# A 12-tile mLSTM attention woven into a mixture of experts: the opening's order on GpSimd and VectorE is changed, and tiles 4 to 11 get two more units between their steps

## The chip, the cores and the metric
The kernel runs on one core of a Trainium2 chip. The metric is the device time of one execution in microseconds (us), as the median of several runs. TensorE (PE) does matmuls and transposes, ScalarE (ACT) activations and copies, VectorE (DVE) elementwise work, GpSimd (POOL) masks and clears, SyncE (SP) starts the DMAs.

## The reference
Three layers follow one another over 1536 tokens (2 batches of 768) with 320 features:

```python
# 1. mLSTM attention, 8 heads of 40, for every step t
m_new = np.maximum(f_gate[:, :, t] + m, i_gate[:, :, t])
f_stab = np.exp(f_gate[:, :, t] + m - m_new)
i_stab = np.exp(i_gate[:, :, t] - m_new)
C = f_stab[:, :, None, None] * C + i_stab[:, :, None, None] * np.einsum('bhd,bhe->bhde', vt, kt)
n = f_stab[:, :, None] * n + i_stab[:, :, None] * kt
y[:, :, t] = o * (C @ q) / np.maximum(np.abs(n . q), 1.0)      # o = sigmoid(o_gate)
# 2. MoE 1: Sinkhorn-normalised gates P (8 rounds), dense over 8 experts
h = np.maximum(x @ w1[e], 0.0);  out += P[:, e:e + 1] * (h @ w2[e])
# 3. MoE 2: the same sizes, top-1 expert of each token by softmax
```

## The kernel before
**Attention in 12 tiles.** Attention is done in its chunked form, in tiles of 128 tokens that alternate between the two batches. `attn(i)` is a Python generator; each `yield` ends one step of a tile. In order, a tile's steps are: `pw`, two matmuls that spread the gates (L239, from a gate tile `gl_` and a tile `R` that VectorE makes in `make_R`, L211), whose result ScalarE turns into the decay weights `W` (relu L244, exp L245) and GpSimd masks (L246); the transposes of q and of k (`turn`, L225, copied out by ScalarE at L229); the scores `sc` (L262); the product of scores and `W` on VectorE (L268); `pn`, weights times v (L274, two steps of four heads each); `pi`, query times state (L291), with the chain `num` on VectorE that divides and gates (L292 to L302); `pc`, the state's increment (L308); the transposes of the tile's result x (L336, L337), copied as a high part `xh` by ScalarE (L341, L345), with the low part `xl` by VectorE (L346, L347); the update of the state `cbd` (L324, L325).

**MoE 1 in items.** The two layers of an expert are split into a high and a low part of each operand, so a product takes three matmuls. An item is one expert on two or four tiles: eight `s1_unit`s (eight matmuls each, L477 to L485, ScalarE's relu `hh` L486, VectorE's `hl` L487) and then `s2_mm` (L492 to L494). Expert weights come in by DMA as `raw` chunks; `split_chunk` makes a high part `w1h` or `w2h` on ScalarE (L461) and a low part `w1l` or `w2l` on VectorE or GpSimd (L465).

**What sets the order.** The program is emitted under a manual schedule: the order of the Python calls is the order on each engine, and an engine takes its instructions in that order. Tiles 0 and 1 (`f0`, `f1`, with `lead=True`) run in the opening by explicit `steps(...)` calls. Tiles 2 to 11 run inside items 0 to 4, which have 144 units; a unit is half an `s1_unit` or six `s2_mm` matmuls. After each unit `bg_early(u)` takes one step of each running generator. A hand-written table gives the unit at which a tile's `pw` is emitted, and `make_R` for it is emitted two units earlier, after the steps of that unit:

```python
AT = {5: 2, 9: 3, 20: 4, 30: 5, 40: 6, 50: 7, 58: 8, 66: 9, 74: 10, 82: 11}
if u + 2 in AT:
    make_R(AT[u + 2])
if u in AT:
    g = attn(AT[u]); next(g); active.append(g)
```

`GT` starts the gate scans of later chunks (`gates(c)`, L146 to L170 on VectorE), `DT` the decays (L180, L187, L188), `OT` the sigmoids of o (`sigmoid_o`: it loads the sigmoid table at L98, does two tiles at L101, and loads the exp table again at L104). `keep_warm(n, cols)` emits n matmuls on zeros that nothing reads. `emit_const` and `emit_const1` clear and mask constants on GpSimd.

Of the kernel before, what the change touches and what calls it, by code (L numbers as in the profile page):

```python
# [18 lines left out]
def mlstm_moe_moe_kernel(ctx, tc, q, k, v, i_gate, f_gate, o_gate, wg1, w1a, w2a, wg2, w1b, w2b, out):  # L19
    nc = tc.nc  # L20
    pe, act, dve, pool, sp = nc.tensor, nc.scalar, nc.vector, nc.gpsimd, nc.sync
# [13 lines left out]
    def f32(ap):  # L35
        return ap.bitcast(F32)
# [46 lines left out]
    gl_ = atp.tile([128, S], F32R, name="gl_")  # L83
# [21 lines left out]
        yield  # L105

    def emit_const():
        pool.memset(mask, 0.0)
        for t in range(4):
            pool.affine_select(out=mask, in_=mask, pattern=[[-1, 2 * H]], compare_op=ALU.not_equal, fill=1.0, base=-32 * t, channel_multiplier=1)  # L110
        pool.memset(ident, 0.0)
        pool.affine_select(out=ident, in_=ident, pattern=[[-1, 128]], compare_op=ALU.not_equal, fill=1.0, base=0, channel_multiplier=1)
        for t in range(2):
            for w in (qs, ks):
                pool.memset(w[t][:, :, D:64], 0.0)
        pool.memset(f32(gl_), 1.0)
        for t in ku:
            pool.memset(t[:, :, D:64], 0.0)
        dve.memset(gx, 1.0)
        dve.memset(wgr2[0:64, 2], 0.0)  # L120
        dve.memset(msk, 1.0)
        dve.memset(msk[:, 0:1], 0.0)
        for t in vs:
            dve.memset(t[:, :, D:D + 1], 1.0)

    def emit_const1():
        for w in (qs, ks):
            pool.memset(w[2][:, :, D:64], 0.0)
        for t in cbd:
            pool.memset(t, 0.0)  # L130
        pool.memset(one, 1.0)
        pool.memset(fold, 0.0)
        for t in range(2):
            pool.affine_select(out=fold, in_=fold, pattern=[[-1, E]], compare_op=ALU.not_equal, fill=1.0, base=-E * t, channel_multiplier=1)
# [41 lines left out]
    def decays(c0, c1):  # L176

        Gv = G.rearrange("p (c t) -> p c t", t=L)
        n = c1 - c0
        dve.tensor_tensor(out=gend[:, c0:c1], in0=Gv[:, c0:c1, L - 1:L].to_broadcast([R16, n, 2 * H]),  # L180
                          in1=mask[0:R16].unsqueeze(1).to_broadcast([R16, n, 2 * H]), op=ALU.mult)
        yield
        yield
        yield
        p = pst()
        for c in range(c0, c1):
            pe.transpose(p[:, (c - c0) * R16:(c - c0 + 1) * R16], G[:, c * L:(c + 1) * L], ident[0:R16, 0:R16])  # L187
        pe.matmul(p[:, 256:256 + n * R16], one, gend[:, c0:c1].rearrange("p c h -> p (c h)"), start=True, stop=True)  # L188
        act.activation(out=dq[:, c0:c1].rearrange("p c h -> p (c h)"), in_=p[:, 0:n * R16], func=AF.Exp)
        act.activation(out=dec[:, c0:c1].rearrange("p c h -> p (c h)"), in_=p[:, 256:256 + n * R16], func=AF.Exp)  # L190
# [4 lines left out]
    def keep_warm(n, cols=512):  # L195

        for _ in range(n):
            pe.matmul(warm_p[:, 0:cols], warm[:, 0:128], warm[:, 0:cols], start=True, stop=True)
# [16 lines left out]
    def attn(i, ps=pst, lead=False):  # L215
# [6 lines left out]
        def turn(src, dst):  # L222
            pq = ps()
            for p in range(4):
                pe.transpose(pq[:, p * L:(p + 1) * L], src[:, 2 * p:2 * p + 2, :].rearrange("s a d -> s (a d)"), ident)  # L225
            if i == 1 and dst is kT:
                dve.tensor_copy(dst.rearrange("p a t -> p (a t)"), pq)
            else:
                act.copy(out=dst.rearrange("p a t -> p (a t)"), in_=pq)  # L229
# [18 lines left out]
        if c < NCH - 1:  # L248
            u = ku[i % 2]
# [4 lines left out]
        if not lead:  # L254
            turn(qs[j], qT)
            yield
            turn(ks[j], kT)
            yield
        sc = [ps(), ps()]
        for p in range(4):  # L260
            for a in range(2):
# [6 lines left out]
            dve.tensor_tensor(out=Wv, in0=sc[a].rearrange("s (p t) -> s p t", t=L), in1=Wv, op=ALU.mult)  # L268
        yield
        yield  # L270
        pn = ps()
        for a in range(2):
            for h in range(a, H, 2):
                pe.matmul(pn[:, h * V:(h + 1) * V], W[:, h, :], vs[j][:, h, :], start=True, stop=True)  # L274
                if lead:
                    keep_warm(1, 256)
            yield
        num = atp2.tile([128, H, V], F32, tag="num", name="num")
        nf = num.rearrange("t h d -> t (h d)")
# [79 lines left out]
    def load_rows(dst, src):  # L359

        sp.dma_start(out=dst[:, 0:2], in_=src[0:256, :].rearrange("(a p) f -> p a f", p=128))
        sp.dma_start(out=dst[0:64, 2], in_=src[256:320, :])
        sp.dma_start(out=dst[64:128, 2], in_=src[256:320, :])
# [4 lines left out]
    def split_wg():  # L368
        act.copy(out=wgs[:, :, 0:E], in_=wgr)
        dve.tensor_tensor(out=wgs[:, :, E:2 * E], in0=wgr, in1=f32(wgs[:, :, 0:E]), op=ALU.subtract)  # L370
# [58 lines left out]
    def load_chunk():  # L429
        n = nload[0]  # L430
        if n >= len(chunks):
            return
        e, w, t = chunks[n]
        r = raw.tile([128, FF], F32, tag="raw", name="raw")
        if w == "w1" and t < 2:
            sp.dma_start(out=r, in_=w1a[e, t * 128:(t + 1) * 128, :])
        elif w == "w1":
            sp.dma_start(out=r[0:64], in_=w1a[e, 256:320, :])
            sp.dma_start(out=r[64:128], in_=w1a[e, 256:320, :])
        else:  # L440
            k0, k1 = 3 * t, min(3 * t + 3, NF)
            sp.dma_start(out=r[:, 0:(k1 - k0) * DM].rearrange("p (k d) -> p k d", d=DM),
                         in_=w2a[e, k0 * 128:k1 * 128, :].rearrange("(k p) d -> p k d", p=128))
        raws[n] = r
        nload[0] += 1

    def split_chunk(eng=None, wait=False):

        n = nsplit[0]
        if n >= len(chunks):  # L450
            return
        e, w, t = chunks[n]
        if eng is None:
            eng = dve if e < 3 else pool
        r = raws.pop(n)
        if w == "w1":
            rv, h, l = r, w1h[:, t, :], w1l[:, t, :]
        else:
            k0, k1 = 3 * t, min(3 * t + 3, NF)
            rv, h, l = r[:, 0:(k1 - k0) * DM].rearrange("p (k d) -> p k d", d=DM), w2h[:, k0:k1, :], w2l[:, k0:k1, :]  # L460
        act.copy(out=h, in_=rv)  # L461
        nsplit[0] += 1

        def low():
            eng.tensor_tensor(out=l, in0=rv, in1=f32(h), op=ALU.subtract)  # L465
            load_chunk()
        if wait:
            return low
        low()
# [519 lines left out]
    with tc.manual_schedule():  # L989
# [15 lines left out]
        load_chunk()  # L1005
        drain(gates(0))
        g1 = gates(1)
        emit_const1()
        alt = [0]

        def psx():
            alt[0] += 1
            return ps1() if alt[0] % 2 else ps2()
        f0, f1 = attn(0, pst, True), attn(1, psx, True)
        make_R(0)
        make_R(1)

        def steps(*fs):
            for f in fs:
                next(f)  # L1020
        steps(f0, f0, f1, f0, f1)
        steps(f0, g1, g1)
        steps(f1)
        steps(f0, f0)
        steps(f1, f1)
        steps(g1, g1)
        low = split_chunk(wait=True)
        for t in range(2):
            act.activation(out=so[t], in_=so[t], func=AF.Sigmoid)
# [1 line left out]
        keep_warm(3)  # L1031
        steps(f0, f0, f0)
        steps(f1)
        low()
        steps(f0)
        keep_warm(2)
        steps(f1, f1, f1)
        steps(f0)
        steps(f1)
        low = split_chunk(wait=True)  # L1040
        steps(f0)
        steps(f1)
        steps(f1)
        low()
        split_chunk()
        keep_warm(2)
        load_tile(3, "o")
        active = [g1, g1]
# [8 lines left out]
        def bg_early(u):  # L1057
            for g in list(active):
                if next(g, "end") == "end":
                    active.remove(g)  # L1060
            if u % 2 == 1 and slow:
                if next(slow[0], "end") == "end":
                    slow.pop(0)
            if u in GT:
                active.append(gates(GT[u]))
            if u in DT:
                active.append(decays(DT[u], DT[u] + 1))
            if u == 8:
                load_rows(wgr, wg1)
                sp.dma_start(out=wgr2[:, 0:2], in_=wg2[0:256, :].rearrange("(a p) f -> p a f", p=128))  # L1070
                sp.dma_start(out=wgr2[64:128, 2], in_=wg2[256:320, :])
            if u == 20:
                split_wg()
            if u in OT:
                active.append(sigmoid_o(OT[u]))
            if u == 3:
                active.extend((f0, f1))
# [3 lines that stand above are left out]
                g = attn(AT[u])  # L1081
                next(g)
                active.append(g)
            for blk, at_ in ((0, 24), (1, 66), (2, 97)):
                if u == at_:
                    active.append(logits(wgs, blk))
            if u == 100:
                slow.append(sinkhorn())

        units = [0]  # L1090
# [100 lines left out]
```

## Time and profile before
| what | value |
|---|---|
| median of 3 runs | 1002.5 us (1001.16 to 1004.19) |
| the profiled execution's own time | 1005.57 us |
| its span in the trace | 1003.9 us |
| TensorE busy | 970.8 us (97%) |
| VectorE busy | 483.0 us (48%) |
| ScalarE busy | 358.0 us (36%) |
| GpSimd busy | 202.7 us (20%) |
| mean granted TensorE clock | 0.985 of full speed |

The busy times are those of the traced span. The granted clock is a share of 2.4 GHz; 0.50 is 1.2 GHz. A row of the timeline has the start, the duration, engine, line, operation, output and input tiles with their shape, and in brackets how long the engine stood idle ahead of it and what released it.

### The profile page before, as it was taken

What the parts mean: (1) busy time and instruction counts of PE and PEld (TensorE: products, weight loads), DVE (VectorE), ACT (ScalarE), POOL (GpSimd) and SP (SyncE); (2) the same over time, 40 slices, a digit from 0 to 9 for tenths busy, and PEclk for the clock granted to TensorE, in tenths of its full rate; (3) what the DMA queues carried; (4) which work ended last, traced back from release to release, by engine and by line L of the source; (5) the groups of instructions that cost most, each with busy time, mean ns of one, the idle gap of its engine ahead of it and who ended that gap; (6) DMA issues with size and microseconds to landing.
All of it is one profiled execution on the core that took longest, in us unless ns stands there. A gap on an engine that the chain in (4) does not pass through costs nothing. (4 is left out here: it accounts for less than half of the span.)

```text
span 1003.9 us, 14450 instructions
## 1 busy us (share of the span) xinstructions
PE 970.8 (97%) x5633; PEld 856.5 (85%) x5633; DVE 483.0 (48%) x1089; ACT 358.0 (36%) x585; POOL 202.7 (20%) x206
## 2 busy tenths in 40 slices
PE   7898999999999999999999999999999998899997
PEld 5888788888999888899998888999888986788885
DVE  8655865565523422222222222222225468687773
ACT  5644565222312232113113211311332134567772
POOL 3212121001000022004002200500221112365552
PEclk9798999999999999999999999999999999899999
DMA  9722621200321405002101200210100034788772
GB/s 196 162 49 37 158 59 50 65 19 1 95 105 55 146 24 182 36 1 61 55 1 35 82 1 1 76 41 1 34 1 27 20 94 133 225 233 245 238 231 76
DMA packets 91366, 84.11 MB, mean 84 GB/s; under 512 B 54237, under 2 KB 81887, under 8 KB 91296
## 3 DMA queue, kind: packets, MB, share of 16 engines
q1 hardware_dynamic: 89088, 76.42, 27.3%
q0 software_dynamic: 2208, 6.75, 1.9%
q8 instruction: 45, 0.74, 0.3%
q14 instruction: 25, 0.20, 0.1%
HBM read 79.21 MB, written 4.76 MB: 84 GB/s over the span
## 5 line engine op out<-in xcount | busy, mean ns | idle before, releaser
L486 ACT ACTIVATE hh<-s 128x512 fp32r<-128x512 f32 (+1 forms) x200 | 116.1, 580 | 446.8 <-PE s L485 446.7
L492 PE MATMUL s<-w2h,hh 128*128 128x320 f32 x832 | 262.7, 316 | 0.0
L493 PE MATMUL s<-w2l,hh 128*128 128x320 f32 x832 | 258.0, 310 | 0.0
L494 PE MATMUL s<-w2h,hl 128*128 128x320 f32 x832 | 258.0, 310 | 0.0
L487 DVE SCALAR_TENSOR_TENSOR hl<-s,hh 128x512 fp32r<-128x512 f32 (+1 forms) x200 | 133.8, 669 | 217.1 <-ACT hh L486 216.7
L492 PEld LDWEIGHTS s<-w2h,hh 128*128 128x128 f32 x832 | 157.2, 189 | 2.0
L493 PEld LDWEIGHTS s<-w2l,hh 128*128 128x128 f32 x832 | 157.2, 189 | 1.5 <-DVE w2l L840 0.2
L494 PEld LDWEIGHTS s<-w2h,hl 128*128 128x128 f32 x832 | 157.0, 189 | 0.0
L534 DVE SCALAR_TENSOR_TENSOR acc<-s,probs,acc 128x320 f32<-128x320 f32 x76 | 41.8, 551 | 188.7 <-PE s L494 188.7
L465 POOL TENSOR_TENSOR w1l<-raw,w1h 128x1024 fp32r<-128x1024 f32 x15 | 35.8, 2418 | 390.3 <-ACT w1h L461 390.3
L477 PE MATMUL s<-xh,w1h 128*128 128x512 f32 (+1 forms) x200 | 79.9, 400 | 0.4 <-DVE es L666 0.4
L482 PE MATMUL s<-xl,w1h 128*128 128x512 f32 (+1 forms) x200 | 79.8, 399 | 0.0
L483 PE MATMUL s<-xh,w1l 128*128 128x512 f32 (+1 forms) x200 | 77.9, 390 | 0.8 <-DVE w1l L465 0.8
L485 PE MATMUL s<-xh,w1l 128*128 128x512 f32 (+1 forms) x200 | 78.1, 390 | 0.6 <-DVE w1l L465 0.6
L478 PE MATMUL s<-xl,w1h 128*128 128x512 f32 (+1 forms) x200 | 77.9, 389 | 0.2 <-DVE xl L346 0.2
L480 PE MATMUL s<-xh,w1h 128*128 128x512 f32 (+1 forms) x200 | 77.7, 388 | 0.0
L484 PE MATMUL s<-xh,w1h 128*128 128x512 f32 (+1 forms) x200 | 77.5, 387 | 0.0
L479 PE MATMUL s<-xh,w1l 128*128 128x512 f32 (+1 forms) x200 | 77.5, 387 | 0.0
L485 PEld LDWEIGHTS s<-xh,w1l 128*128 128x128 f32 x200 | 38.2, 191 | 9.4 <-DVE w1l L465 0.8
L477 PEld LDWEIGHTS s<-xh,w1h 128*128 128x128 f32 x200 | 38.2, 191 | 9.0 <-DVE es L666 0.8
L483 PEld LDWEIGHTS s<-xh,w1l 128*128 128x128 f32 x200 | 38.1, 190 | 8.9 <-DVE w1l L465 1.0
L480 PEld LDWEIGHTS s<-xh,w1h 128*128 128x128 f32 x200 | 38.1, 191 | 8.5
(303 smaller groups left out, 1428.8 us busy)
## 6 DMA issues: line engine op xcount, KB each, us to landing
raw<-in_moe_w_dram SPq DMA_DIRECT2D x44, 320.0 KB, 3.3
raw<-in_moe_w_dram SPq DMA_DIRECT2D x54, 256.0 KB, 4.2
w2raw<-in_moe_w_dram SPq DMA_DIRECT2D x17, 640.0 KB, 5.4
raw<-in_moe_w_dram SPq DMA_DIRECT2D x20, 512.0 KB, 3.6
raw<-in_moe_w_dram SPq DMA_DIRECT2D x20, 480.0 KB, 3.8
wr<-in_moe_w_dram SPq DMA_DIRECT2D x8, 1024.0 KB, 8.3
q<-in_q_dram SPq DMA_DIRECT2D x12, 160.0 KB, 3.8
k<-in_k_dram SPq DMA_DIRECT2D x12, 160.0 KB, 3.9
```

Source lines behind the costliest of these rows:

```text
L477: pe.matmul(p, w1h[:, 0, fs], xh_[:, 0, cols], start=True, stop=False)
L478: pe.matmul(p, w1h[:, 0, fs], xl_[:, 0, cols], start=False, stop=False)
L479: pe.matmul(p, w1l[:, 0, fs], xh_[:, 0, cols], start=False, stop=False)
L480: pe.matmul(p, w1h[:, 1, fs], xh_[:, 1, cols], start=False, stop=False)
L482: pe.matmul(p, w1h[:, 1, fs], xl_[:, 1, cols], start=False, stop=False)
L483: pe.matmul(p, w1l[:, 1, fs], xh_[:, 1, cols], start=False, stop=False)
L485: pe.matmul(p, w1l[:, 2, fs], xh_[:, 2, cols], start=False, stop=True)
L486: act.activation(out=hh[:, ft, 0:n], in_=p, func=AF.Relu)
L487: dve.scalar_tensor_tensor(out=hl[:, ft, 0:n], in0=p, scalar=0.0, in1=f32(hh[:, ft, 0:n]), op0=ALU.max, op1=ALU.subtract)
L492: pe.matmul(p[:, 0:DM], hh[:, ft, ts], w2h[:, ft, :], start=(first and ft == 0), stop=False)
L493: pe.matmul(p[:, 0:DM], hh[:, ft, ts], w2l[:, ft, :], start=False, stop=False)
L494: pe.matmul(p[:, 0:DM], hl[:, ft, ts], w2h[:, ft, :], start=False, stop=(ft == NF - 1))
```

## The change
`gl_` is cleared first on GpSimd instead of after the pads; `emit_const1` (clears of tile 2's pads, of the states, and a small mask) moves behind the weight masks of tiles 0 and 1; the gate steps of chunk 1 that stood between the two tiles' products, and the low parts of the first weight chunks, take other places in the opening; the matmuls on zeros inside the two lead tiles' `pn` are left out. Tiles 4 to 11 get one more empty step ahead of `sc` and one more ahead of `pn`, so all their later steps come one and then two units later. The logits and the Sinkhorn rounds start two units later.

```diff
     def emit_const():
+        pool.memset(f32(gl_), 1.0)
         pool.memset(mask, 0.0)
...
-        pool.memset(f32(gl_), 1.0)
...
             turn(ks[j], kT)
             yield
+            if i > 3:
+                yield
         sc = [ps(), ps()]
...
         yield
         yield
+        if i > 3:
+            yield
         pn = ps()
         for a in range(2):
             for h in range(a, H, 2):
                 pe.matmul(pn[:, h * V:(h + 1) * V], W[:, h, :], vs[j][:, h, :], start=True, stop=True)
-                if lead:
-                    keep_warm(1, 256)
...
         g1 = gates(1)
-        emit_const1()
...
         steps(f1)
+        emit_const1()
         steps(f0, f0)
         steps(f1, f1)
-        steps(g1, g1)
         low = split_chunk(wait=True)
...
         steps(f1)
+        steps(f0)
         low()
-        steps(f0)
         keep_warm(2)
         steps(f1, f1, f1)
         steps(f0)
         steps(f1)
+        split_chunk()
+        steps(f0)
         low = split_chunk(wait=True)
-        steps(f0)
         steps(f1)
         steps(f1)
         low()
-        split_chunk()
...
-            for blk, at_ in ((0, 24), (1, 66), (2, 97)):
+            for blk, at_ in ((0, 24), (1, 68), (2, 99)):
...
-            if u == 100:
+            if u == 102:
                 slow.append(sinkhorn())
```

The line numbers in the rows of the changed order below are one to two higher than in the kernel before (L270 is the product of L268, L278 the `pn` of L274, L338 the transposes of L336, L348 the low part of L346, L467 that of L465, L494 to L496 the matmuls of L492 to L494).

VectorE in the opening, from the products of tiles 0 and 1 to the third low part, before:

```order
L268 TENSOR_TENSOR W<-a,W 128x4x128 x2
L156 TENSOR_TENSOR acc<-acc 16x128
L158 SCALAR_TENSOR_TENSOR acc<-acc 16x128
L268 TENSOR_TENSOR W<-s_309,W 128x4x128
L268 TENSOR_TENSOR W<-s_310,W 128x4x128
L465 TENSOR_TENSOR w1l<-raw,w1h 128x1024
L286 COPY num<-a 128x8
```

And with the change:

```order
L270 TENSOR_TENSOR W<-a,W 128x4x128 x2
L270 TENSOR_TENSOR W<-s_309,W 128x4x128
L270 TENSOR_TENSOR W<-s_310,W 128x4x128
L288 COPY num<-a 128x8
L289 TENSOR_TENSOR num<-a,o_102 128x8x40
L297 SCALAR_TENSOR_TENSOR den<-num 128x8
L298 TENSOR_SCALAR den<-den 128x8
L299 RECIPROCAL den<-den 128x8
L301 TENSOR_TENSOR x<-num,den 128x320
L467 TENSOR_TENSOR w1l<-raw,w1h 128x1024
```

The two gate steps (L156, L158) have gone from between the products, and the first low part stands behind tile 0's chain instead of ahead of it. The second low part, which stood behind both tiles' `xl`, now stands ahead of them, and the third alone behind them.

TensorE around tile 9's `pw` (unit 66, the L239 row), before; the L336 and L337 rows are the transposes of tile 7's x, the L274 rows tile 8's `pn`:

```order
L336 MATMUL a<-ident,x 128x128 x2
...
L274 MATMUL a<-v_101,W 128x41 x4
L492 MATMUL s_1507<-w2h,hh 128x320
L493 MATMUL s_1507<-w2l,hh 128x320
L494 MATMUL s_1507<-w2h,hl 128x320
L492 MATMUL s_1507<-w2h,hh 128x320
L493 MATMUL s_1507<-w2l,hh 128x320
L494 MATMUL s_1507<-w2h,hl 128x320
L274 MATMUL a<-v_101,W 128x41 x4
L239 MATMUL a<-R,gl__110 128x512 x2
```

And with the change, at the same unit; the L338 row is the first of the transposes of tile 7's x:

```order
L338 MATMUL a<-ident,x 128x128 x2
L339 MATMUL a<-ident,x 64x128
L494 MATMUL s_1476<-w2h,hh 128x320
...
L494 MATMUL s_1476<-w2h,hh 128x320
L495 MATMUL s_1476<-w2l,hh 128x320
L496 MATMUL s_1476<-w2h,hl 128x320
L239 MATMUL a<-R,gl__110 128x512 x2
L494 MATMUL s_1476<-w2h,hh 128x320
L495 MATMUL s_1476<-w2l,hh 128x320
L496 MATMUL s_1476<-w2h,hl 128x320
```

Tile 8's `pn` has gone behind tile 9's `pw`, and the transposes of tile 7's x, which stood four units ahead of that `pw`, stand two units ahead of it: twelve matmuls of MoE 1 are all that is left between them.

VectorE over the same units, before, from tile 7's low part to the R of tile 9:

```order
L346 TENSOR_TENSOR xl_69<-a,xh_66 128x2x128
L347 TENSOR_TENSOR xh_66<-a,xh_66 64x128
L156 TENSOR_TENSOR acc<-acc 16x128
L487 SCALAR_TENSOR_TENSOR hl<-s_1474,hh 128x512
L325 TENSOR_TENSOR cbd_107<-cbd_107,a 40x4x41 x2
L268 TENSOR_TENSOR W<-a,W 128x4x128 x2
L158 SCALAR_TENSOR_TENSOR acc<-acc 16x128
L160 CAST gx<-acc 16x128
L211 TENSOR_TENSOR R<-gx,mask 128x1024
```

And with the change:

```order
L348 TENSOR_TENSOR xl_69<-a,xh_66 128x2x128
L349 TENSOR_TENSOR xh_66<-a,xh_66 64x128
L270 TENSOR_TENSOR W<-a,W 128x4x128 x2
L160 CAST gx<-acc 16x128
L211 TENSOR_TENSOR R<-gx,mask 128x1024
```

Tile 7's low part, tile 8's product and tile 9's R now stand in one unit (64), one right behind the other.

## Rows read from the trace of the kernel before
**Rows 1.** The page: busy time of the engines, share of the span, instructions.
```profile
PE 970.8 (97%) x5633; PEld 856.5 (85%) x5633; DVE 483.0 (48%) x1089; ACT 358.0 (36%) x585; POOL 202.7 (20%) x206
```
**Rows 2.** Waits of TensorE, 76 to 190 us: total, times, longest.
```profile
PE a L274 <- issue: 2.0, 3, 1.1
PE a L274 <- DVE W L268: 2.0, 3, 1.1
PE a L239 <- ACT W L244: 1.5, 2, 0.7
PE a L262 <- ACT kT L229: 1.2, 2, 0.8
```
**Rows 3.** Timeline of VectorE in the opening.
```profile
4.86 0.92 DVE L160 CAST gx<-acc 16x128 fp32r<-16x128 f32 x1
...
13.50 0.52 DVE L156 TENSOR_TENSOR acc<-acc 16x128 f32<-16x128 f32 x1
14.05 0.41 DVE L158 TENSOR_TENSOR_SCAN acc<-acc 16x128 f32<-16x128 f32 x1
...
22.67 2.36 DVE L465 TENSOR_TENSOR w1l<-raw,w1h 128x1024 fp32r<-128x1024 f32 x2
24.95 0.21 DVE L160 CAST gx<-acc 16x128 fp32r<-16x128 f32 x1
...
28.16 1.22 DVE L211 TENSOR_TENSOR R<-gx,mask 128x1024 fp32r<-128x1024 f32 x1
```
**Rows 4.** Timeline of GpSimd: the clears of the states in `emit_const1`.
```profile
5.02 0.69 POOL L130 MEMSET cbd<- 128x328 f32 x2
```
**Rows 5.** Timeline of TensorE in the opening.
```profile
25.08 0.58 PE L485 MATMUL s<-xh,w1l 128*128 128x256 f32 x1 [0.62 <-DVE w1l L465]
...
29.43 0.72 PE L239 MATMUL a<-R,gl__110 128*128 128x512 f32 x2 [0.63 <-DVE R L211]
```
**Rows 6.** Windows: us, busy of PE, PEld, DVE, ACT, POOL; granted clock; DMA.
```profile
15.00:25.00 10.00, 8.36 (x74) 7.08 (x72) 8.46 (x22) 5.43 (x10) 0.00 (x0) 1.00 1.07 199
25.00:28.20 3.20, 3.12 (x14) 3.12 (x15) 2.13 (x10) 0.77 (x2) 0.00 (x0) 0.50 1.14 266
35.40:42.00 6.60, 6.45 (x27) 5.59 (x27) 4.53 (x10) 5.21 (x11) 2.60 (x5) 0.50 0.39 90
86.30:93.10 6.80, 6.80 (x32) 6.69 (x31) 3.60 (x9) 0.38 (x1) 0.00 (x0) 0.50 0.00 0
```
**Rows 7.** Timeline of TensorE, tiles 9 to 11.
```profile
137.67 1.06 PE L274 MATMUL a<-v,W 128*128 128x41 f32 x8 [1.12 <-DVE W L268]
...
165.33 0.38 PE L336 MATMUL a<-ident,x 128*128 128x128 f32 x2
...
165.81 0.30 PE L493 MATMUL s<-w2l,hh 128*128 128x320 f32 x1
...
166.38 0.31 PE L494 MATMUL s<-w2h,hl 128*128 128x320 f32 x1
...
171.47 0.71 PE L239 MATMUL a<-R,gl__110 128*128 128x512 f32 x2
```
**Rows 8.** Timeline of VectorE: tile 9's low part to tile 11's R.
```profile
166.41 0.43 DVE L346 TENSOR_TENSOR xl<-a,xh 128x256 fp32r<-128x256 f32 x1 [3.48 <-ACT xh L345]
...
167.15 0.66 DVE L325 TENSOR_TENSOR cbd<-cbd,a 40x164 f32<-40x164 f32 x2
167.82 1.29 DVE L268 TENSOR_TENSOR W<-a,W 128x512 f32<-128x512 f32 x2
169.03 1.22 DVE L211 TENSOR_TENSOR R<-gx,mask 128x1024 fp32r<-128x1024 f32 x1
```
**Rows 9.** Timeline of ScalarE: weights of tile 5, load of the exp table.
```profile
76.03 0.60 ACT L244 ACTIVATE W<-a 128x512 f32<-128x512 f32 x1 [2.17 <-PE a L239]
...
77.85 0.63 ACT L245 ACTIVATE W<-W 128x512 f32<-128x512 f32 x1
...
167.54 1.28 ACT L104 ACT_TABLE_LOAD   x1
```

## The prediction
> **What bounds the kernel now.** The page comes first: TensorE is busy 97% of the span, VectorE 48%, ScalarE 36%, GpSimd 20% [rows 1]. So time is lost or won where TensorE idles or runs at half its clock. Its waits come next. From 76 us to 190 us, the stretch of tiles 5 to 11, four kinds of wait make 6.7 us: `pn` with no releaser shown (2.0), `pn` for the product of scores and weights (2.0), the scores for the copy of kT (1.2) and `pw` for the relu of the `pw` ahead of it (1.5) [rows 2]. In the opening it waits for VectorE's third `w1l` (0.62) and for tile 2's R (0.63) [rows 5]. The windows show what those waits do to the clock: 25.0 to 28.2 us, 35.4 to 42.0 us and 86.3 to 93.1 us run at 0.50, that is at 1.2 GHz [rows 6], so up to 1.6, 3.3 and 3.4 us are lost there (half of each stretch, since the same matmuls take half as long at 2.4 GHz).
>
> All of the change lies in the first 190 us. What is gained or lost there moves the end by as much, since MoE 1 runs on TensorE from there on.
>
> **The opening.** Four edits act on VectorE, which is the engine that TensorE waits for here.
> (1) The cast L160 of chunk 0 takes 0.92 us at 4.86 while GpSimd clears the states at 5.02 (0.69 us), and 0.21 us at 24.95 with nothing on GpSimd [rows 3, 4]. With `emit_const1` moved away, the gate chain, R and `pw` start earlier by some 0.5 us (the cast's 0.71, of which about 0.2 lay under the scan ahead of it in the pipeline; estimate).
> (2) L156 and L158 (0.52 and 0.41) leave the place between the products [rows 3]. They come back behind the third `w1l`, ahead of tile 2's R. Tile 1's product then waits for GpSimd's mask instead, so I take 0.7 at that point, not 0.93.
> (3) The pair of low parts (2.36 for two, so 1.18 each [rows 3]) no longer stands whole behind tile 1's `xl`. The second fits in while VectorE waits for x of tile 1; this brings the third forward by 1.18.
> (4) On the other side tile 0's chain now waits for the sigmoids, which ScalarE still makes at the same place, and tile 1's copy `xh` waits behind one more `w1h` cast.
> Followed row by row with the durations of before, the third `w1l` ends at 23.4 us instead of 25.03, and R of tile 2 at about 28.4 instead of 29.38 (28.16 + 1.22 [rows 3]), because the two gate steps now lie ahead of it. So the sum for the opening is -1.0 us. Its bounds: -2 if the chain moves by all of (1) and (3), and +0.5 from contention, as the moved clears would now run beside tile 0's product and chain, whose cost is bounded below by nothing and above by the 0.71 of edit (1).
>
> Leaving out sixteen matmuls on zeros costs TensorE nothing in itself; they stand where it would wait for VectorE anyway, which is busy 8.46 of 10 us there [rows 6]. But they are activity. In 15 to 25 us TensorE was busy 8.36 of 10 us at clock 1.00 and the clock fell to 0.50 only at 25.0 [rows 6]. The Trainium skill ("TensorE: Matmul & The Clock Gate", Part 1) says that the throttled clock is the default and activity releases it, which speaks against leaving them out. No row of before shows the opening without them. If the clock falls some microseconds sooner, the x transposes and the first matmuls of item 0 run at half clock: about +1.5 us by the 1.6 of the stretch that is there now. I put nothing into the sum and +1.5 into the range.
>
> Of the moved clears the skill has another rule ("SBUF — State Buffer", SBUF: two separate sides): VectorE with two inputs in SBUF is blocked only by a GpSimd operation that reads SBUF. By it the clears, which only write, would cost the chain's two-input steps nothing, and the opening would be -1.0 either way; that L160, a one-input cast, was slowed by clears [rows 3, 4] agrees with its other half.
>
> **The extra steps of tiles 4 to 11.** What they remove: the waits of `pn` and of the scores, 2.0 + 2.0 + 1.2 = 5.2 us of the 6.7 [rows 2], since the copies and the product get one more unit, about 0.9 us (six matmuls at 0.14, from 165.81 to 166.38 for four [rows 7]).
>
> What they add follows from the offsets. A tile's product comes at AT+6 instead of AT+5, its x transposes at AT+14 instead of AT+12. AT itself is not moved, and R for tile i+1 is still made two units ahead of its `pw`.
> - **Tiles 9 to 11.** AT is spaced by 8 there. So x of tile i-1 (AT+14 of that tile), the product of tile i (AT+6) and R of tile i+1 (AT-2) all fall into one unit, in this order on VectorE. `pw` of tile i+1 is two units later. The chain has been traced: x transposes of tile 9 start at 165.33 [rows 7], then `xh`, `xl` at 166.41, the state's 0.66, the product, and R ends at 170.25 (169.03 + 1.22) [rows 8]; without the state's addition, which moves behind, 4.92 - 0.66 = 4.26 us. In before TensorE had four units and two halves of `pn` to do meanwhile, and arrived at `pw` at 171.47 [rows 7]. Now it has the transposes (0.35) and twelve matmuls (12 x 0.143 = 1.72, or eight of `s1`, about 1.87), 2.1 us. It then waits 4.26 - 2.1 = 2.1 us. For tile 10 the decays' matmuls lie between (about 0.4): 1.7. For tiles 9 and 11 the exp table's load (1.28, just behind the second sigmoid [rows 9]) now stands on ScalarE directly ahead of `xh`, and holds it by 0.7 to 1.1: 3.2 and 2.8. Together 7.7 us. In exchange `pn`'s waits there go (1.12 at 137.67 [rows 7], and three more of 0.2 to 0.6, 2.2 in all).
> - **Tiles 4 to 6.** Spacing is 10. The chain `num` of tile i now comes one unit after `pw` of tile i+1 (AT+11), where ScalarE has four activations of `W` to do, 76.03 to 78.48 [rows 9], and MoE 1's `hh` stands behind them, `hl` behind that, `num` behind `hl`. So the x transposes, which had no wait before, wait: 1.0 to 1.3 us each by hand, 3.6 for three.
> - **Tile 8** comes at a spacing of 8 behind 7, and its `pw` meets the same chain in part: 1.4. Some waits stay (0.9 of tile 5's `pn`, 0.3 around tile 6, 0.4 at a k turn): 1.6.
> Sum of the waits after: 7.7 + 3.6 + 1.4 + 1.6 = 14.3, against 6.7. Waits in a row are not fully additive, since TensorE's standing still lets ScalarE and VectorE catch up; I take 2 off: +5.5. Bounds: +3 (each of the R waits 1.5 smaller, as with a shorter hold by the table) and +8.
>
> The logits and Sinkhorn rounds move by two units and still end ahead of unit 143; SyncE's loads move by one or two units with what precedes them. Nothing waits for either, so I cost them at nothing; without that slack each unit would be some 0.9 us.
>
> **Sum.** -1.0 + 5.5 = +4.5 us. The profiled execution took 1005.57 us, 3.1 above the median, so by it 1010.1; against the median of 1002.5, on which I forecast, 1007.0.
>
> **Rivals.**
> - **The waits just go** (faster). If the R chain is ready in time (in before, `pw` of tile 11 came 1.2 us after its R, 171.47 [rows 7] against 170.25), the change gives -5.2, the clock stays up in 86 to 93 us (-3.4) and the opening gives -1.0: 1002.5 - 9.6 = 993. With half of it, 998. Against it stands the arithmetic of two units. The point from which it decides is whether twelve matmuls can last longer than the chain of 4.26.
> - **Offsets cancel** (no change). The x waits are half as long and the table load does not hold `xh`: the waits after are 8 to 9 us, the opening takes 1 off: 1002 to 1004.
> - **The clock falls too** (slower still). The waits of about 3 us are followed by falls to 0.50, as the shorter ones of before seem to be, each stretch costing 1.6 to 3.4 [rows 6]. Against it: TensorE has more than 10 us of work between two such waits. With one or two more: 1009 to 1014.
> - **Only the opening counts** (the extra steps trade like for like, but the clock falls sooner without the zeros): 1002.5 + 1.5 - 1.0 = 1003.
>
> **How the numbers follow.** About 0.3%, 3 us, is what a measurement of this kernel can tell from no change: below 999.5 is faster, above 1005.5 slower. The new waits as forecast hold 0.45, with their own range of 1003 to 1010; the clock falling too 0.10; cancelling 0.17 and the opening alone 0.08; the waits just going, whole or in half, 0.20. Slower takes the third case and three quarters or more of the forecast, 0.50 in sum; no change the rest of it and the two middling ones, 0.30; faster 0.20. The range reaches from half of the first rival, 997, to the upper end of the third, 1013.
>
> **What would show it.** Right: `pw` (L239) waiting for R in three or four places with some 2 to 3 us each near 134 to 165 us; x transposes waiting for x of tiles 4 to 6; no wait of `pn` for the product in tiles 9 to 11; the last L485 of the first `s1_unit` near 23.5 us instead of 25.08, L160 in 0.2 us. Wrong: R ready ahead of `pw` in tiles 9 to 11, or a clock of 1.00 all through 80 to 100 us.

## The result and the profile after

The changed kernel takes 1015.61 us (median of 4, 1011.32 to 1016.14) against 1001.99 us before (4 runs): a ratio of 1.0123, interval 1.0091 to 1.0156. Measured once more among the experiments, it took 1010.75 us against 1002.02 us, ratio 1.0077 (1.0046 to 1.0107). It is slower, as was forecast, by 13.6 and 8.7 us between the medians (about 12 and 8 us by the ratios) where 4.5 were forecast. The first median lies above the stated range (997 to 1013), the second in it. Every difference in this document is below 2% of the time; a gain or a loss is called one only where its interval leaves out 1.

The profiled execution, of 1011.32 us, is the fastest of the first four. Its page, with the busy times beside those of [rows 1]:

```profile
span 1009.5 us, 14416 instructions
...
PE 971.1 (96%) x5615; PEld 858.1 (85%) x5617; DVE 481.3 (48%) x1089; ACT 358.8 (36%) x585; POOL 203.0 (20%) x206
```

The waits of TensorE from 5 to 200 us (total, times, longest), which answer to [rows 2]:

```profile
PE a L239 <- DVE R L211: 11.7, 6, 3.3
PE a L338 <- DVE x L304: 3.6, 3, 1.3
PE a L264 <- ACT kT L229: 1.3, 1, 1.3
PE a L278 <- DVE W L270: 1.1, 1, 1.1
PE s L480 <- DVE xl L348: 0.8, 1, 0.8
PE a L278 <- issue: 0.7, 1, 0.7
```

From 76 to 190 us alone, the stretch of [rows 2], they are:

```profile
PE a L239 <- DVE R L211: 9.3, 4, 3.3
PE a L338 <- DVE x L304: 3.6, 3, 1.3
PE a L278 <- issue: 0.7, 1, 0.7
PE a L225 <- ACT qT L229: 0.2, 1, 0.2
```

The reader is to see that in this stretch `pn` (now L278) and the scores (L264) hardly wait any more, and that two waits have come in: `pw` for R, 9.3 us there and 11.7 us in all, and the x transposes (L338) for x, 3.6 us. The timeline of TensorE has the places:

```profile
23.77 0.41 PE L487 MATMUL s<-xh,w1l 128*128 128x256 f32 x1 [0.61 <-DVE w1l L467]
28.68 0.72 PE L239 MATMUL a<-R,gl__110 128*128 128x512 f32 x2 [1.11 <-DVE R L211]
...
79.35 0.44 PE L338 MATMUL a<-ident,x 128*128 128x128 f32 x2 [1.27 <-DVE x L304]
...
120.83 0.73 PE L239 MATMUL a<-R,gl__110 128*128 128x512 f32 x2 [1.43 <-DVE R L211]
...
132.54 0.38 PE L338 MATMUL a<-ident,x 128*128 128x128 f32 x2
...
138.09 0.70 PE L239 MATMUL a<-R,gl__110 128*128 128x512 f32 x2 [3.31 <-DVE R L211]
...
155.92 0.72 PE L239 MATMUL a<-R,gl__110 128*128 128x512 f32 x2 [1.69 <-DVE R L211]
...
177.42 1.02 PE L239 MATMUL a<-R,gl__110 128*128 128x512 f32 x2 [2.88 <-DVE R L211]
```

Two rows answer to [rows 5]: the last matmul of the first `s1_unit` comes at 23.77 instead of 25.08, and tile 2's `pw` at 28.68 instead of 29.43. The others are the new waits. What tile 9's `pw` (138.09) waits for is seen on ScalarE and VectorE, which answer to [rows 8, 9]:

```profile
132.35 0.46 ACT L101 ACTIVATE o<-o 128x320 f32<-128x320 f32 x1
132.82 1.28 ACT L104 ACT_TABLE_LOAD   x1
134.11 0.37 ACT L343 CAST xh<-a 128x256 fp32r<-128x256 f32 x1
```
```profile
4.89 0.21 DVE L160 CAST gx<-acc 16x128 fp32r<-16x128 f32 x1
...
13.72 1.29 DVE L270 TENSOR_TENSOR W<-s,W 128x512 f32<-128x512 f32 x2 [0.59 <-POOL wl L251]
...
22.49 1.23 DVE L467 TENSOR_TENSOR w1l<-raw,w1h 128x1024 fp32r<-128x1024 f32 x1
...
27.41 1.23 DVE L211 TENSOR_TENSOR R<-gx,mask 128x1024 fp32r<-128x1024 f32 x1
...
134.67 0.42 DVE L348 TENSOR_TENSOR xl<-a,xh 128x256 fp32r<-128x256 f32 x1 [1.18 <-ACT xh L347]
...
135.40 1.29 DVE L270 TENSOR_TENSOR W<-a,W 128x512 f32<-128x512 f32 x2
...
136.74 1.21 DVE L211 TENSOR_TENSOR R<-gx,mask 128x1024 fp32r<-128x1024 f32 x1
```

Tile 7's x is transposed at 132.54. Its copy `xh` stands behind the load of the exp table until 134.11; the low part, tile 8's product and R follow without a gap until 137.95. TensorE has done its twelve matmuls by 134.8. The first four VectorE rows answer to [rows 3]: the cast of chunk 0 takes 0.21 instead of 0.92, tile 1's product waits for GpSimd's `wl` and not for gate steps, the third low part ends at 23.72 instead of 25.03, tile 2's R at 28.64 instead of 29.38.

The granted clock (the third number from the end of a row, 1.00 or about 0.50; ahead of it stand the stretch and the busy times of PE, PEld, DVE, ACT and POOL), which answers to [rows 6], in the profile after and in that of the second measurement:

```profile
86.00:93.00 7.00, 7.00 (x56) 6.84 (x55) 2.26 (x4) 4.19 (x9) 2.75 (x4) 1.00 0.01 2
157.00:167.50 10.50, 10.50 (x49) 10.50 (x48) 0.00 (x0) 5.09 (x9) 1.27 (x2) 0.51 0.00 0
177.50:181.00 3.50, 3.50 (x12) 2.92 (x12) 1.99 (x4) 2.82 (x6) 1.05 (x2) 0.52 0.31 96
```
```profile
134.50:148.50 14.00, 12.67 (x54) 12.36 (x55) 6.87 (x12) 5.71 (x9) 2.28 (x5) 0.51 0.27 71
175.00:189.50 14.50, 13.42 (x49) 12.04 (x50) 6.54 (x10) 6.09 (x10) 1.27 (x2) 0.53 0.26 74
```

The stretch of 86 to 93 us, at 0.50 before, runs at 1.00. In its place the clock is at 0.5 behind the waits for R of tiles 9 to 11: in the one execution behind the second and the third, in the other from the first and from the third on. Not every wait is followed by a fall: in the first execution the longest, 3.31 us ahead of tile 9's `pw`, is followed by a clock of 1.00 until 157 us.

The same window in five profiled executions, the stretch in which tiles 8 to 11 run: before, the change, the change again, the steps alone, and the change with these waits filled (the last two are experiments below).

```profile
120.00:195.00 75.00, 72.47 (x495) 62.93 (x495) 47.51 (x99) 37.81 (x70) 10.58 (x18) 1.00 0.26 64
120.00:195.00 75.00, 66.29 (x431) 59.88 (x431) 40.47 (x82) 35.21 (x62) 10.68 (x18) 0.91 0.21 52
120.00:195.00 75.00, 67.11 (x407) 60.84 (x407) 37.36 (x77) 33.65 (x60) 9.67 (x18) 0.82 0.20 50
120.00:195.00 75.00, 64.66 (x413) 58.25 (x413) 39.83 (x82) 34.97 (x64) 10.68 (x18) 0.89 0.26 63
120.00:195.00 75.00, 73.64 (x493) 62.90 (x497) 43.13 (x90) 36.36 (x64) 10.60 (x18) 0.98 0.19 51
```

Of the 75 us the clock took nothing before, 7, 13.5 and 8 us with both steps, and 1.5 us with the waits filled (75 times what the clock lacks to 1). In the profiles of the other nine kernels below it took nothing there in six, and 3.8 us in three: the clears alone and each of the two steps alone.

**Two numbers for each kernel.** Every run lists its span and its mean granted clock. Span times clock is about what the span would be at full clock ("full-clock span"), and span times (1 - clock) about what the clock took ("clock loss"). As an example, 1009.5 x 0.985 = 994.4 and 15.1 for the run profiled. This is an approximation: within one kernel, the span grew by 0.65 to 0.95 us for each us of clock loss, probably because some waits shrink when TensorE is slow. So each us of clock loss lowers the full-clock span by 0.05 to 0.35 us, and two kernels with unlike clock loss can be compared by it only within that. The means over the runs, with 9 to 12 runs of a kernel (8 of the steps alone, 4 of the first measurement) and 27 to 35 of the kernel before beside them, are uncertain by about 0.5 us (full-clock span) and 1 to 1.5 us (clock loss). Left out of these means as slow are one execution of the kernel before in each of two groups (1010.85 and 1010.68 us) and one of the step ahead of sc (3339.19 us). The experiments ran in three groups, on three chips, each with the kernel before beside it. The ratio is taken without these three, and differs by up to 0.2% from the quotient of the two medians.

| kernel | us | before beside it | ratio (95%) | full-clock span | clock loss | before: the two |
|---|---|---|---|---|---|---|
| change, first | 1015.61 | 1001.99 | 1.0123 (1.0091 to 1.0156) | 993.2 | 19.8 | not listed |
| change, again | 1010.75 | 1002.02 | 1.0077 (1.0046 to 1.0107) | 992.9 | 15.6 | 990.4, 8.9 |
| opening alone | 998.4 | 1003.04 | 0.9939 (0.991 to 0.9969) | 988.9 | 7.6 | 989.7, 11.3 |
| steps alone | 1015.57 | 1003.04 | 1.0112 (1.0071 to 1.0153) | 993.8 | 19.8 | 989.7, 11.3 |
| change, R early | 997.55 | 1003.04 | 0.9932 (0.9895 to 0.9969) | 987.7 | 9.1 | 989.7, 11.3 |
| change, R waits filled | 1004.25 | 1003.04 | 1.0002 (0.9973 to 1.0031) | 994.7 | 8.0 | 989.7, 11.3 |
| opening, zeros kept | 1000.53 | 1003.39 | 0.9971 (0.9943 to 0.9998) | 990.0 | 8.7 | 989.6, 11.1 |
| zeros left out alone | 1002.7 | 1003.39 | 1.0013 (0.9979 to 1.0047) | 989.1 | 11.3 | 989.6, 11.1 |
| clears alone | 1004.3 | 1003.39 | 0.9992 (0.996 to 1.0023) | 990.0 | 11.0 | 989.6, 11.1 |
| R early, x later | 997.11 | 1003.39 | 0.995 (0.9924 to 0.9975) | 984.6 | 11.3 | 989.6, 11.1 |
| the same, filled | 995.39 | 1002.02 | 0.9941 (0.991 to 0.9972) | 986.5 | 7.1 | 990.4, 8.9 |
| step ahead of sc alone | 1002.58 | 1002.02 | 1.0012 (0.9978 to 1.0047) | 986.5 | 13.7 | 990.4, 8.9 |
| step ahead of pn alone | 999.03 | 1002.02 | 0.9965 (0.993 to 1.0) | 986.6 | 9.5 | 990.4, 8.9 |

### The profile page after: what moved, and what is told of

It reads as the page before. It is cut to its first block, busy times and chain, and to the rows that moved or that the text cites. A ratio compares the mean times of both kernels' runs of the same rounds, so it can differ in the third digit from the quotient of the medians.

```text
span 1009.5 us, 14416 instructions
## 1 busy us (share of the span) xinstructions
PE 971.1 (96%) x5615; PEld 858.1 (85%) x5617; DVE 481.3 (48%) x1089; ACT 358.8 (36%) x585; POOL 203.0 (20%) x206
## 5 line engine op out<-in xcount | busy, mean ns | idle before, releaser
L494 PE MATMUL s<-w2h,hh 128*128 128x320 f32 x832 | 263.1, 316 | 0.0
L496 PE MATMUL s<-w2h,hl 128*128 128x320 f32 x832 | 258.5, 311 | 0.0
L494 PEld LDWEIGHTS s<-w2h,hh 128*128 128x128 f32 x832 | 157.4, 189 | 1.8
L496 PEld LDWEIGHTS s<-w2h,hl 128*128 128x128 f32 x832 | 157.3, 189 | 0.0
L467 POOL TENSOR_TENSOR w1l<-raw,w1h 128x1024 fp32r<-128x1024 f32 x15 | 35.8, 2413 | 389.0 <-ACT w1h L463 389.0
L487 PEld LDWEIGHTS s<-xh,w1l 128*128 128x128 f32 x200 | 38.4, 192 | 9.4 <-DVE w1l L467 0.8
L486 PEld LDWEIGHTS s<-xh,w1h 128*128 128x128 f32 x200 | 38.2, 191 | 8.5
L479 PEld LDWEIGHTS s<-xh,w1h 128*128 128x128 f32 x200 | 38.1, 190 | 8.5 <-DVE es L668 0.8
L482 PEld LDWEIGHTS s<-xh,w1h 128*128 128x128 f32 x200 | 38.0, 190 | 8.5
```

The source lines that it names most:

```text
L479: pe.matmul(p, w1h[:, 0, fs], xh_[:, 0, cols], start=True, stop=False)
L482: pe.matmul(p, w1h[:, 1, fs], xh_[:, 1, cols], start=False, stop=False)
L486: pe.matmul(p, w1h[:, 2, fs], xh_[:, 2, cols], start=False, stop=False)
L487: pe.matmul(p, w1l[:, 2, fs], xh_[:, 2, cols], start=False, stop=True)
L494: pe.matmul(p[:, 0:DM], hh[:, ft, ts], w2h[:, ft, :], start=(first and ft == 0), stop=False)
L496: pe.matmul(p[:, 0:DM], hl[:, ft, ts], w2h[:, ft, :], start=False, stop=(ft == NF - 1))
```

## The experiments

**The two halves apart.** The opening's edits without the extra steps, and the extra steps with the opening of before:

```diff
# opening alone: the change without these four lines
-            if i > 3:
-                yield
         sc = [ps(), ps()]
...
-        if i > 3:
-            yield
         pn = ps()
# steps alone: the kernel before with these four lines added
```

The start of the logits and of the Sinkhorn rounds goes with the steps: two units later in the steps alone, as before in the opening alone.

> The opening's edits alone, without the extra steps of tiles 4 to 11. Theory A (the extra steps make the waits on R and x, and the waits make the granted clock fall): 1001 us, between 999 and 1003, no wait of pw for R above 1.5 us. Rival B (leaving out the matmuls on zeros lets the clock fall more often in the opening and after it): 1006 to 1010 us.

> The extra steps of tiles 4 to 11 alone, the opening as before. Theory A: 1013 to 1017 us, pw waits for R by about 3.3, 1.7 and 2.9 us for tiles 9 to 11, and the clock is at 0.50 somewhere behind them. Rival B: 1006 to 1009 us, the waits alone.

The opening alone makes the kernel faster by 4.6 us, a little more than theory A expected (and tile 2's `pw` waits 2.01 us for R in its profile, where 1.5 was the most expected), the steps alone slower by 12.5, as expected of theory A. At full clock that is -0.8 and +4.1; the clock loss falls by 3.7 with the one and grows by 8.5 with the other. The steps carry the whole loss, and some two thirds of it is clock. Not all of that clock loss need lie behind the waits for R: the profiled execution of the steps alone lost about 8 us from 120 to 195 us, and about 10 us ahead of 60 us, where the program is that of before.

**R two units earlier.** The whole change, with `make_R` of tiles 8 to 11 moved ahead of the copies of x and the product:

```diff
-            if u + 2 in AT:
-                make_R(AT[u + 2])
+            ahead = 4 if u >= 50 else 2
+            if u + ahead in AT:
+                make_R(AT[u + ahead])
```

> The whole change, with R of tiles 8 to 11 made four units ahead of its pw instead of two, so ahead of the x copies and the product on VectorE. Theory A: the waits of pw for R of tiles 8 to 11 (about 9.3 us) go, the clock falls behind them go too, the x waits of tiles 4 to 6 stay: 1001 to 1005 us. Rival C (R is not what bounds there, the product or the copies are waited for next): 1010 us or more, with the idle time under another name.

The time falls by 13 to 18 us, to 997.55. The waits of TensorE, 5 to 200 us:

```profile
PE a L338 <- DVE x L304: 3.6, 3, 1.3
PE a L239 <- DVE R L211: 3.5, 3, 2.0
...
PE a L239 <- DVE xh L349: 1.2, 2, 0.8
```

None of the three waits for R that remain is of tiles 8 to 11 (they are of `pw` of tiles 0, 2 and 4); the next thing there is a wait of 1.2 us in two places for the last reader of x's transposes. So the order of three operations on VectorE is the cause of the waits for R of tiles 8 to 11, and not TensorE's shorter distance in itself. The full-clock span is below that of before by 2.0, and below the change by 5.2 to 5.5. The expectation was too high by 3.5 us.

**The waits filled, not shortened.** The whole change, and ahead of `pw` of tiles 9 to 11 matmuls on zeros that nothing reads:

```diff
             pw = ps()
+            if g == 0 and i >= 9:
+                for _ in range(7 if i == 10 else 12):
+                    pe.matmul(pw, warm[:, 0:128], warm, start=True, stop=True)
```

> The whole change, with matmuls on zeros ahead of pw of tiles 9 to 11 (12, 7 and 12 of 512 columns) that fill the wait for R; the wait itself is not shortened. Theory A, its part on the clock: the clock stays at 1.00 behind these places and the time falls by the 5 to 7 us that the stretches at half clock cost, to 1008 to 1011 us. Rival D (the clock falls for another reason): 1015 us as with the change.

It takes 1004.25, some 6 to 11 us less than the change, with more work, and less than the 1008 to 1011 expected. Its clock loss is 8.0 instead of 15.6 to 19.8. (Its full-clock span is 1.5 to 1.8 longer; a clock loss that is 8 to 12 us smaller can make that much by the approximation alone.) Three rows and a window of its trace; the first is the transposes of tile 7's x, and of the twelve matmuls on zeros the trace holds eleven:

```profile
133.38 0.38 PE L341 MATMUL a<-ident,x 128*128 128x128 f32 x2
...
136.29 2.76 PE L241 MATMUL a<-warm 128*128 128x512 bf16 x11 [0.66 <-DVE xh L352]
138.86 0.73 PE L242 MATMUL a<-R,gl__110 128*128 128x512 f32 x2
```
```profile
124.00:190.00 66.00, 64.75 (x452) 55.14 (x454) 39.29 (x80) 32.34 (x57) 9.30 (x16) 1.00 0.22 57
```

`pw` comes no sooner (5.5 us behind the transposes, as in the change: 132.54 to 138.09), and the clock is at 1.00 throughout the stretch in which the change loses it. Just ahead of that, behind the wait of 1.43 us for R of tile 8, which was not filled, it fell in this trace too: 0.57 from 120 to 124 us. What takes the clock there is thus that TensorE stands idle in those waits.

**The zeros and the clears.** The opening alone with the sixteen matmuls on zeros kept; before without them; and before with GpSimd's clears alone in the new order:

```diff
# opening alone, zeros kept
+                if lead:
+                    keep_warm(1, 256)
# the kernel before, zeros left out
-                if lead:
-                    keep_warm(1, 256)
# the kernel before, clears moved
     def emit_const():
+        pool.memset(f32(gl_), 1.0)
...
-        pool.memset(f32(gl_), 1.0)
...
         g1 = gates(1)
-        emit_const1()
...
         steps(f1)
+        emit_const1()
```

> The opening's edits alone, but with the sixteen matmuls on zeros kept inside the lead tiles' pn. Theory A2 (the opening gains by VectorE's order, the zeros only hold TensorE back a little): 998 to 1000 us, span times granted clock up by 0 to 0.6 us against the opening alone. Rival B2 (the better clock of the opening alone comes from leaving the zeros out): clock back at 0.989, 1002 us.

> The kernel before, only without the sixteen matmuls on zeros. Theory A2: tile 1's chain no longer waits 0.57 us for pn, the rest as before: 1002 to 1003 us, clock 0.989. Rival B2: clock 0.992 or more and 999 us. Rival E (the skill's rule, less activity lets the clock fall sooner): clock under 0.987, 1005 us or more.

> The kernel before with only GpSimd's clears in the new order. Theory A2: the cast of chunk 0 takes about 0.2 us instead of 0.92, the first pw comes some 0.5 us sooner, and little of it reaches the third low part: 1002 us, span times clock 0 to 0.5 us less. If the clears carried the opening's gain: 999 us.

Without the zeros alone the time does not change, and neither does the clock loss (11.3 against 11.1). The clears alone change no time either (1004.3 where 1002 was expected, ratio 0.9992), though the cast takes 0.22 us in that trace. The opening with the zeros kept takes 1000.53, a little more than expected, and is 1.1 us longer at full clock than without them. Neither the zeros nor the clears alone carry the opening's gain. At full clock all these differences from before, -0.8 to +0.4, are hardly larger than their uncertainty of 0.4 to 0.7. The traces are sharper: the third low part ends at 25.03 before, at 23.95 with the new order and the zeros kept, at 24.34 with the zeros alone left out, at 23.72 with the change. So the new order on both engines gives about 1.1 us at that place, and the absence of the zeros some 0.2 to 0.7.

**x one unit later, and the other waits filled.** The change with R early and one empty step more ahead of the x transposes of tiles 4 to 6; then the same with matmuls on zeros in the four longest waits left:

```diff
+        if 4 <= i <= 6:
+            yield
         transpose_x(x, i, ps, act)
# and then, filled (fill(p, n): n matmuls on zeros of 512 columns into p)
             pw = ps()
+            if g == 0:
+                fill(pw, {2: 9, 4: 5}.get(i, 0))
...
         pn = ps()
+        fill(pn, {3: 4, 5: 7}.get(i, 0))
```

> The whole change with R of tiles 8 to 11 four units ahead, and one more empty step ahead of the x transposes of tiles 4 to 6. Theory A: the three waits for x (3.6 us) go, and what falls of the clock follow them go too: 993 to 996 us. Rival F (something else waits there next, the state or the product): 997 to 999 us, the idle time under another name.

> The kernel with R of tiles 8 to 11 four units ahead and x of tiles 4 to 6 one unit later, with matmuls on zeros of 512 columns in its four longest waits that are left: 9 ahead of pw of tile 2, 5 ahead of pw of tile 4, 4 ahead of pn of tile 3, 7 ahead of pn of tile 5. Theory A (a wait costs its length, and a second time by the clock): span times clock the same within 1 us, clock up from 0.989 to 0.993 or more, 993 to 995 us. Rival D (the falls of the clock do not hang on what TensorE does in the waits): 997 us, clock 0.989.

The first has the shortest full-clock span of all, 984.6, 5.0 below before; but its clock loss is 11.3, and of the gain over the version ahead of it 0.4 us are left: 997.11, in the range of rival F and not of theory A. The waits of its trace:

```profile
PE a L239 <- DVE R L211: 4.1, 3, 2.0
PE a L278 <- DVE W L270: 3.3, 3, 1.6
PE a L239 <- DVE xh L351: 1.2, 2, 0.8
```

The x waits are gone, and `pn` waits for the product again, up to 1.6 us. Filled, the clock loss is 7.1 instead of 11.3, against 8.9 of the runs of before beside it, and the full-clock span is 1.9 longer, of which the approximation alone can make 0.2 to 1.5. At 995.39, close to what theory A expected, and a ratio of 0.9941 it beats both kernels, as do the two versions with R early and the opening alone; between these four the intervals tell nothing apart.

**One extra step at a time**, in the kernel before:

```diff
# ahead of sc alone
+            if i > 3:
+                yield
         sc = [ps(), ps()]
# ahead of pn alone
+        if i > 3:
+            yield
         pn = ps()
```

The logits and Sinkhorn rounds start as before in both.

> The kernel before, with the empty step ahead of sc alone in tiles 4 to 11. The product then stands in the unit in which R of the next tile is made, the x transposes one unit ahead of it. Theory A: pw of tiles 9 to 11 waits for R by 0.5 to 1.5 us each, and pn's waits go: 1003 to 1007 us.

> The kernel before, with the empty step ahead of pn alone in tiles 4 to 11. The x transposes then stand in the product's unit, and R one unit behind. Theory A: pw of tiles 9 to 11 waits for R by 0.8 to 2 us each, the scores' waits stay: 1004 to 1009 us, between before and the whole change.

Both were expected slower and neither is. At full clock each is 3.8 to 3.9 us shorter than before, whereas both together are 4.1 longer. The step ahead of sc gains no time by it, since its clock loss is 13.7 against 8.9 (and 0.2 to 1.7 of its 3.9 can be the approximation). TensorE's rows with a wait for R of tiles 9 to 11, with the step ahead of sc:

```profile
135.63 0.74 PE L239 MATMUL a<-R,gl__110 128*128 128x512 f32 x2 [0.59 <-DVE R L211]
...
170.56 0.73 PE L239 MATMUL a<-R,gl__110 128*128 128x512 f32 x2 [0.47 <-DVE R L211]
```

and with the step ahead of pn:

```profile
133.20 0.84 PE L239 MATMUL a<-R,gl__110 128*128 128x512 f32 x2 [1.77 <-DVE R L211]
...
153.46 0.73 PE L239 MATMUL a<-R,gl__110 128*128 128x512 f32 x2 [0.77 <-DVE R L211]
...
168.13 0.73 PE L239 MATMUL a<-R,gl__110 128*128 128x512 f32 x2 [0.88 <-DVE R L211]
```

With one step, only two of the three operations share a unit: product and R, or x and product. The waits for R are 1.1 and 3.4 us in sum, against 7.9 with both steps; with the step ahead of sc tile 10's `pw` does not wait at all, otherwise each is within or near what was expected. What the expectation missed is what the steps remove elsewhere, which is then larger than this: all waits of TensorE from 76 to 190 us come to 6.9 us before, and to 4.6 and 4.8 us with one step.

**The change once more:**

> The whole change once more, beside the others. Theory A: 1015 us, clock 0.980, and falls of the clock to 0.50 behind the R waits of tiles 9 to 11 in the profile. If 1005 to 1010 us, the first measurement caught a run of bad executions.

It is slower again, by less. The full-clock span is the same as in the first measurement (992.9 and 993.2); all of the difference is in the clock loss, 15.6 and 19.8 (uncertain by 1.2 and 1.6).

## Why the prediction was wrong, and where it was right

**The bound.** Right for the waits: they lie in the first 190 us, and the waits of TensorE name them. From tile 11's `pw` to the end of the span both profiled executions take the same, 832.4 us before (1003.9 - 171.47) and 832.1 after (1009.5 - 177.42). The clock also falls after 800 us, where nothing was changed (5.7 us of clock loss before and 1.9 after, from 800 to 990 us), so single executions can differ by that alone.

**The opening.** The rows moved as forecast: the third low part ends at 23.72 (forecast 23.4), R of tile 2 at 28.64 (28.4), `pw` is 0.75 sooner. The cast's 0.92 fell to 0.21. The size at full clock, forecast -1.0, came out at -0.8 with the opening alone, uncertain by about 0.6, so it is not shown closely. One cost was put at nothing and is not: the zeros. Before, tile 1's chain waited for the `pn` in which they stand:

```profile
18.86 0.17 DVE L286 COPY num<-s 128x8 f32<-128x8 f32 x1 [0.57 <-PE s L274]
```

With the zeros alone left out, in an execution whose clock was at 1.00 there, tile 2's `pw` comes at 28.37 with the old order on VectorE, in the profile of the opening alone at 28.28. How much of the 0.75 at `pw` is the order, how much the zeros and how much the clock is therefore open. The moved clears ran from 14.43 us on (the states' at 14.83) beside tile 1's product, which took 1.29 instead of the 1.25 of before, and were over when tile 0's chain began at 15.65 or soon after. So the bound of 0.5 us from contention was not needed. The Trainium skill's rule on two-input steps ("SBUF — State Buffer", SBUF: two separate sides) speaks of no loss either, but its case, clears beside the chain, hardly came up.

That the clock falls sooner without the zeros did not happen: the clock loss without them is that of before, 11.3 against 11.1 (uncertain by 1.6 and 0.8). The Trainium skill's rule that activity releases the throttle ("TensorE: Matmul & The Clock Gate", Part 1) is neither confirmed nor contradicted by that. But the opening alone lost 3.7 us less to the clock than before, and that stood nowhere in the forecast. Its cause is open: with the zeros kept 2.4 of it are left (both uncertain by about 1.2), and neither the clears nor the zeros alone give any. The order on VectorE alone was not tried.

**The waits of tiles 4 to 11.** Right one by one. R was forecast late by 1.4, 3.2, 1.7 and 2.8 us for tiles 8 to 11 and was late by 1.43, 3.31, 1.69 and 2.88; x of tiles 4 to 6 by 1.0 to 1.3 each, 3.6 in all, and the view says 3.6 in three places. The table load ahead of `xh`, the twelve matmuls and the 4.26 us of the chain were all as read (for tile 10, which has no table load, x transposes at 151.60, R's end at 155.87: 4.27). All waits from 76 to 190 us come to 13.8 us, forecast 14.3. Turned into time, 14.3 against 6.7 were taken as +5.5. The steps alone gave +4.1 at full clock, the whole change +2.5 against the runs beside it where +4.5 was forecast; but 8.5 and 6.7 us more of clock loss lower these by 0.4 to 3.0 and 0.3 to 2.3, so that +5.5 and +4.5 are not refuted. The two profiled executions, whose clock loss happens to be the same (15.1), differ by 5.75 us: forecast from that trace 1010.1, measured 1011.32. The sum of the waits was thus not what failed.

**The step that failed is the clock.** The sum has no term for it: the prediction took half-clock stretches as before, gave their growth a chance of 0.10 and argued "TensorE has more than 10 us of work between two such waits". Measured, the steps alone lost 8.5 us more to the clock, and the change 6.7 more than the runs beside it; in the profiles with both steps 7 to 13.5 us are lost from 120 to 195 us, where that of before lost nothing. The argument did not hold: TensorE has that work, and in the second profile the clock was still at 0.51 from 134.5 to 148.5 us, with TensorE busy 12.67 of 14 us. The third rival is the case that came: 1010.75 lies in its 1009 to 1014, 1015.61 above it, since a stretch cost not 1.6 to 3.4 us but up to 7 (half of 14 us). That the idling itself is the cause, and not some other effect of the steps, is shown by the filled waits: no shorter way to `pw`, and 8.0 us of clock loss instead of 15.6 to 19.8.

A second slip: the clock of before was read from one trace, whose own loss (0.985 of 1003.9, so 15.1) was above the mean of before (8.9 to 11.3). And one sign was badly chosen. A clock of 1.00 all through 80 to 100 us was to show the forecast wrong; it came, and the kernel was slower all the same, since the clock fell elsewhere. As far as single profiles can tell, the fall there went with the steps: the clock from 86 to 93 us is 0.50 to 0.76 in three of the five profiles without extra steps (before, the opening with zeros kept, the clears alone), and 1.00 from 62 to 118 us in all nine with one or both.

**The faster rival** ("the waits just go") was wrong for the change, but its gain in full-clock span is what either step brings alone, and the whole change becomes faster than before once R is made earlier (997.55, ratio 0.9932).

## What to carry to other kernels

Before a stream of a software pipeline is shifted by whole units, list for each unit what then falls into it on the slowest side engine: here two operations in one unit made waits for R of 1.1 and 3.4 us in sum and no loss of time, three made waits of 1.7 to 3.3 us a tile, and moving the one producer that could be emitted earlier (R) turned the loss into a gain. An idle stretch of the matmul engine can be paid twice, for its length and by the clock: the steps alone cost some 4 us at full clock and 8.5 us of clock loss. So a forecast has to price both, and the clock over many executions rather than from one trace. Where a wait can't be scheduled away, matmuls that nothing reads are worth trying in it; the sixteen in the lead tiles' `pn` brought no time that could be measured.

## What was not expected of the hardware

The clock is granted differently from execution to execution of one kernel. The 62 runs of the kernel before beside the first eight experiments range from a mean clock of 0.982 to 0.998 and from 995 to 1009 us. The kernel without the zeros had about the same waits as before (3.9 and 3.1 us for R and for the product from 5 to 200 us, before 3.6 and 3.1) in a profiled execution that kept 1.00 all through this stretch:

```profile
5.00:200.00 195.00, 178.09 (x1298) 157.18 (x1297) 133.38 (x296) 102.44 (x193) 39.40 (x70) 1.00 0.43 100
```

So a wait of 1 to 2 us, and by the 3.31 us ahead of tile 9's `pw` even a longer one, does not decide a fall. That waits make a fall more likely is what the means of the filled and the unfilled kernels show, and one trace tells little of what the clock will cost on average. The span and the clock of each run do, when they are taken apart.
